# Threshold attention and two FFN layers on one core: value products of later batches moved behind a pair's last tile

## The chip, the cores and the metric

The kernel runs on one core of a Trainium2 chip. The metric is the device time of the whole program in microseconds. Three runs of the kernel before gave a median of 1142.88 us (1142.81 to 1144.38). Besides, one execution was profiled; all rows below come from it.

## The reference, cut to what matters

Four batches of eight heads, 576 positions, 64 channels a head; then two feed-forward layers over 2304 tokens, 512 wide inside and 2048 hidden.

```
scores = scale * q @ k.T                       # per batch and head: 576 x 576
thresh = max(scores, -1) - tau
scores = where(scores >= thresh, scores, -1e9)
attn   = softmax(scores)                       # over the keys
x      = attn @ v                              # 576 x 64 per head, heads side by side: 2304 x 512
h = x @ w_in;  x = (max(h,0) + alpha*min(h,0)) @ w_out
h = x @ w2_in; out = (h * clip(h+3, 0, 6) / 6) @ w2_out
```

## The kernel before

**Attention.** Heads go in pairs, 16 pairs, four to a batch. A pair has nine tiles (`NT = 9`): tile t = 0 to 7 holds 128 queries of one head (head 0 and head 1 in turn), tile 8 the last 64 queries of both. For each tile `do_S` makes the scores (line 377, tile name `s`), `soft` takes the maximum on VectorE, the exponential on ScalarE (`e`) and the threshold with the sum on VectorE, and after each odd tile and after tile 8 `soft_norm` divides on GpSimd and `do_T` transposes the weights on TensorE (`t` at line 439, `r` for the last 64 keys at line 430). ScalarE copies each transpose from PSUM to SBUF (lines 440 and 431, into `p`, or `p1` for tile 8). `do_PV` multiplies with the values (line 470, `pv`), ScalarE copies the product from PSUM to `xo` (line 476), and behind tile 8 DMAs store `xo`.

`do_T` and `do_PV` call 128 queries of both heads a unit; a pair has four units and the 64 queries of tile 8. Before the change one `p` tile holds two units and there are two buffers. In batch 0 each unit is multiplied as soon as it is transposed. In the later batches there are two places per pair: behind tile 3 the first two units (256 columns), behind tile 8 the other two (256 columns) and the 64 of tile 8, side by side in one PSUM tile. Each value product at line 470 is ten matmuls over the keys, which the trace shows as 20 instructions, since the operands are float32. Scores and the FFN run in float32r (shown as f32 too).

**FFN.** Blocks of 512 tokens, one per batch, 16 groups `h` (line 216, 12 matmuls of 512 columns) and 16 groups `o` (lines 245 and 251, also 12 each) per layer. ScalarE, VectorE and GpSimd turn `h` into `m`, `g` and the two halves `gs`, and split the weights into two halves `wi` and `wo`; in the first pass through a layer they also decode them from float64 (lines 148 to 154).

**What sets the order.** The program is written as one loop over the 144 tiles; from three tiles behind batch 0 on, groups of the FFN queue are added at a fixed pace, about 1.8 a tile. A scheduler then puts the instructions of each engine in an order, by priorities: the steps of a tile stand 50 places higher, `do_PV` of batch 0 100 places. Each engine works through its list in order. PSUM is split into `ps_s` (scores, two tiles), `ps_t` (transposes, two banks) and `ps_ho` with two banks, in which `pv`, `h`, `o` and some `pt` (transposes of q and k, line 322) take turns in the order in which the program is written. So a value product keeps its place among the FFN groups, while scores and transposes may run ahead of it as far as `e` (four buffers) and `p` allow.

Behind the last pair the rest of the queue runs, and then a last FFN stage over batch 3 and the left-over queries, with six PSUM banks for `o` and two for `h`.

Of the kernel before, what the change touches and what calls it, by code (L numbers as in the profile page):

```python
# [9 lines left out]
F32 = mybir.dt.float32  # L10
# [9 lines left out]
P = 128  # L20
# [12 lines left out]
def kernel(  # L33
# [13 lines left out]
    nc = tc.nc  # L47
    B, H, S, D = q.shape
# [4 lines left out]
    SM = 512  # L53
    SR = S - SM
# [364 lines left out]
    def do_T(n, t, first):  # L419
        e, _ = st["e"]  # L420
        if n == 1:
            pt = a3.tile([P, 1, NB + 1, P], F32, tag="p1", name="p1", bufs=1)
        elif t % 4 == 1:
            pt = a3.tile([P, 2, 2 * NB + 1, P], F32, tag="p", name="p", bufs=2)
        else:
            pt = st["p"][0]
        dst = pt[:, t % 4 // 2 if n == 2 else 0]
# [15 lines left out]
        st["p"] = st.get("p", []) * (t % 4 != 1) + [pt] * (n == 1 or t % 4 == 1)  # L443


    def do_PV(i):
# [3 lines left out]
        if b == 0:  # L450
            parts = [(1, st["p"][1], 0)] if t == NT - 1 else [(2, st["p"][0], t % 4 // 2)]
        elif t in (3, NT - 1):
            parts = [(2, st["p"][0], None)] + [(1, p1, 0) for p1 in st["p"][1:]]
        else:
            return
        pv = ps_ho.tile([P, SM], F32, tag="ho", name="pv")
        at = 0
        for n, pt, u in parts:
            m = SR if n == 1 else P if u is not None else 2 * P
            for kt in range(NB + 1):  # L460
                for h in (1, 0) if b == 0 else (0, 1):
                    blk = n * NB if kt == NB else kt + NB * h * (n - 1)
                    o = pv[64 * h:64 * h + 64, at:at + m]
                    if n == 1:
                        r = pt[:, 0, blk, SR * h:SR * h + m]
                    elif u is None:
                        o, r = o.rearrange("p (u q) -> p u q", u=2), pt[:, :, blk, :]
                    else:
                        r = pt[:, u, blk, :]
                    nc.tensor.matmul(o, lhsT=vn[:, h, kt, :], rhs=r, start=(kt == 0 and at == 0), stop=(kt == NB), skip_group_check=True)  # L470
            at += m
        if "xo" not in st[pi]:
            st[pi]["xo"] = a2.tile([P, S], F32, tag="xo", name="xo")
        xo = st[pi]["xo"]
        end = S if t == NT - 1 else t // 2 * P + P
        nc.scalar.copy(xo[:, end - at:end], pv[:, 0:at])
# [237 lines left out]
```

## Time and profile before

| | before |
|---|---|
| median of three runs | 1142.88 us |
| the profiled execution: time, span | 1142.49 us, 1140.7 us |
| TensorE (PE) matmul busy | 1099.5 us, 96% of the span |
| VectorE (DVE), ScalarE (ACT), GpSimd (POOL) busy | 609.1, 692.3, 682.5 us |
| granted TensorE clock, mean | 0.998 |
| value products, line 470, 1120 instructions | 90.0 us busy |

The time is read off TensorE: where another engine is late, TensorE stands still, and where it does not stand still the time is the sum of what its matmuls take from start to start. Batch 0 alone takes the first 117 us or so, the mixture of attention and FFN lasts to about 845 us, and the last stage of the FFN takes the rest.

### The profile page before, as it was taken

To read this page: it belongs to the slowest core of one execution; us is meant where nothing else is said; L and a number is where in the kernel's file an instruction comes from. 1 tells how busy PE (TensorE), PEld (TensorE's weight loads), DVE (VectorE), ACT (ScalarE), POOL (GpSimd) and SP (SyncE) were. 2 spreads that over 40 slices of the span, in tenths; PEclk is the share of its full clock that TensorE was granted. 3 is DMA by queue.
4 is the path that set the end of the run, shared out by engine and by line. 5 is a ranking of instruction groups with operands and counts; after the bars stand their busy time and mean duration, and the time that the engine had idled before them with its cause. 6 is when DMAs were issued, how large, how long until landed. Compare 5 with 4: busy or idle time off the path is not lost.

```text
span 1140.7 us, 18515 instructions
## 1 busy us (share of the span) xinstructions
PE 1099.5 (96%) x6464; PEld 909.3 (80%) x6464; DVE 609.1 (53%) x1215; ACT 692.3 (61%) x1316; POOL 682.5 (60%) x726
## 2 busy tenths in 40 slices
PE   6888999999999999999999999999999999999997
PEld 5677788787777788888878888887778888888886
DVE  6889778988897535463555445362334222232121
ACT  6899889888887655466656565564444333344332
POOL 3877779988888755556556656454344434344432
PEclk9999999999999999999999999999999999999999
DMA  5536456666765432333333432322234222212201
GB/s 166 170 114 202 118 166 223 217 213 208 224 217 177 143 103 85 106 106 98 105 107 116 150 95 64 102 65 85 82 101 160 65 65 65 66 56 65 65 28 56
DMA packets 92765, 137.44 MB, mean 120 GB/s; under 512 B 19328, under 2 KB 48512, under 8 KB 92672
## 3 DMA queue, kind: packets, MB, share of 16 engines
q1 hardware_dynamic: 92672, 136.26, 39.6%
q8 instruction: 51, 0.84, 0.3%
q14 instruction: 42, 0.34, 0.1%
HBM read 101.72 MB, written 25.17 MB: 111 GB/s over the span
## 4 chain that ended last, share of the span: by engine, by line
PE 80%; ACT 6%; DVE 5%; DMA 3%; issue 3%; POOL 2%; SPq 0%; POOLq 0%; DVEq 0%; ACTq 0%
PE h L216 32%; PE o L245 14%; PE o L251 14%; PE pv L470 6%; PE s L377 5%; PE t L439 4%; PE r L251 2%; PE r L245 2%; DVE nmx L398 1%; PE pt L322 1%; ACT e L399 1%; DVE e L401 1%; ACT p L440 1%; DMA raw<-in_k_dram 1%; DMA wo<-f 1%
## 5 line engine op out<-in xcount | busy, mean ns | idle before, releaser
L216 PE MATMUL h<-x,wi 128*128 128x512 f32 (+1 forms) x1536 | 357.3, 381 | 1.7 <-DVE thr L400 1.7
L216 PEld LDWEIGHTS h<-x,wi 128*128 128x128 f32 x1536 | 271.7, 188 | 56.1 <-ACT wi L101 1.9
L241 POOL TENSOR_TENSOR gs<-g,gs 128x512 fp32r<-128x512 f32 (+1 forms) x160 | 192.9, 1207 | 161.8 <-ACT gs L237 160.0
L251 PE MATMUL o<-wo,gs 128*128 128x512 f32 x768 | 193.6, 396 | 3.4 <-DVE g L231 1.5
L245 PE MATMUL o<-gs,wo 128*128 128x512 f32 x768 | 194.2, 397 | 0.3
L251 PEld LDWEIGHTS o<-wo,gs 128*128 128x128 f32 x768 | 140.6, 188 | 35.7 <-DVE g L231 2.9
L245 PEld LDWEIGHTS o<-gs,wo 128*128 128x128 f32 x768 | 140.1, 188 | 29.1 <-DVE g L223 0.9
L231 DVE SCALAR_TENSOR_TENSOR g<-m,h 128x512 f32<-128x512 f32 x80 | 50.6, 632 | 163.5 <-ACT m L229 159.7
L399 ACT ACTIVATE e<-s,nmx 128x576 f32<-128x576 f32 x144 | 107.8, 753 | 48.7 <-DVE nmx L398 47.9
L401 DVE SCALAR_TENSOR_TENSOR e<-s,thr,e 128x576 f32<-128x576 f32 x144 | 116.0, 814 | 37.9 <-ACT e L399 36.9
L223 DVE SCALAR_TENSOR_TENSOR g<-m,rest_sb,h 128x512 f32<-128x512 f32 x80 | 55.4, 693 | 145.0 <-ACT m L221 134.1
L102 POOL TENSOR_TENSOR wi<-st,wi 128x512 fp32r<-128x512 f32 x56 | 72.3, 1292 | 100.4 <-ACT wi L101 100.3
L398 DVE TENSOR_REDUCE nmx<-s 128x1 f32<-128x576 f32 x144 | 106.9, 751 | 45.3 <-PE s L377 44.9
L413 POOL TENSOR_SCALAR e<-e,rc 128x576 f32<-128x576 f32 x144 | 113.2, 798 | 28.7 <-DVE rc L410 25.4
L237 ACT CAST gs<-g 128x512 fp32r<-128x512 f32 (+1 forms) x160 | 93.4, 584 | 34.3 <-DVE g L231 13.1
L229 ACT ACTIVATE m<-h,three 128x512 f32<-128x512 f32 x80 | 51.7, 647 | 102.6 <-PE h L216 100.8
L377 PE MATMUL s<-ka,qt 128*128 128x288 f32 x512 | 97.6, 318 | 7.6 <-DVE thr L400 3.1
L101 ACT CAST wo<-st 128x512 fp32r<-128x512 f32 x96 | 57.3, 620 | 75.2 <-DMA st<-wo 62.8
L221 ACT ACTIVATE m<-h 128x512 f32<-128x512 f32 x80 | 44.5, 556 | 92.9 <-PE h L216 92.4
L102 POOL TENSOR_TENSOR wo<-st,wo 128x512 fp32r<-128x512 f32 x56 | 74.4, 1347 | 39.9 <-ACT wo L101 39.7
L440 ACT COPY p<-t 128x512 f32<-128x512 f32 x144 | 83.3, 598 | 23.3 <-PE t L439 12.4
L470 PE MATMUL pv<-p,v 128*64 128x256 f32 (+2 forms) x1120 | 90.0, 310 | 4.4 <-ACT p L440 4.0
(88 smaller groups left out, 1599.1 us busy)
## 6 DMA issues: line engine op xcount, KB each, us to landing
st<-wi SPq DMA_DIRECT2D x96, 256.0 KB, 2.7
st<-wo SPq DMA_DIRECT2D x96, 256.0 KB, 2.7
raw<-in_moe_w_in_dram SPq DMA_DIRECT2D x32, 512.0 KB, 4.3
raw<-in_moe_w_out_dram SPq DMA_DIRECT2D x32, 512.0 KB, 3.8
ka<-ka SPq DMA_DIRECT2D x30, 304.0 KB, 4.2
wi<-f SPq DMA_DIRECT2D x32, 256.0 KB, 3.0
wo<-f SPq DMA_DIRECT2D x32, 256.0 KB, 3.2
raw<-in_k_dram SPq DMA_DIRECT2D x16, 256.0 KB, 4.1
```

What stands on the lines that cost most here:

```text
L102: lo_eng.tensor_tensor(out=lo, in0=src, in1=f32(hi), op=ALU.subtract)
L216: nc.tensor.matmul(h[:, :n], lhsT=w[:, ws, kt * P:(kt + 1) * P], rhs=x[:, xs, kt, :n], start=(i == 0), stop=(i == len(steps) - 1))
L241: nc.gpsimd.tensor_tensor(out=gs[:, 1, :n], in0=g[:, :n], in1=f32(gs[:, 0, :n]), op=ALU.subtract)
L245: nc.tensor.matmul(o[:, :n], lhsT=w[:, ws, dt * P:(dt + 1) * P], rhs=gs[:, gsel, :n], start=fresh and start and i == 0, stop=stop and i == ...
L251: nc.tensor.matmul(o[:m, :], lhsT=gs[:, gsel, tt * P:tt * P + m], rhs=w[:, ws, :], start=start and i == 0, stop=stop and i == 2)
L377: nc.tensor.matmul(ps[:, half, 0:SH], lhsT=w, rhs=s["k"][:, a, c + half * SH:c + half * SH + SH], start=(n == 0), stop=(n == len(mms) - 1))
L398: nc.vector.tensor_reduce(out=nmx, in_=ps, axis=AX.XY, op=ALU.max, negate=True)
L399: nc.scalar.activation(eh, ps, AF.Exp, bias=nmx, scale=1.0)
L401: nc.vector.scalar_tensor_tensor(out=eh, in0=ps, scalar=thr, in1=eh, op0=ALU.is_ge, op1=ALU.mult, accum_out=sm[:, h:h + 1])
L413: nc.gpsimd.tensor_scalar(out=eh, in0=eh, scalar1=rc[:, h:h + 1], scalar2=0.0, op0=ALU.mult, op1=ALU.add)
L440: nc.scalar.copy(dst[:, h * NB:h * NB + NB], ps)
L470: nc.tensor.matmul(o, lhsT=vn[:, h, kt, :], rhs=r, start=(kt == 0 and at == 0), stop=(kt == NB), skip_group_check=True)
```

## The change

`p` becomes one tile with all four units of a pair, in one buffer instead of two of half the size. In batch 0 the products stay where they are. In later batches the first three pairs of each batch have no product behind tile 3 any more; behind tile 8 they multiply all four units at once, 512 queries in one PSUM bank, and the 64 of tile 8 in a second bank. The last pair of each batch keeps its product behind tile 3, and takes a second bank for the 64 of tile 8 too. Both products of tile 8 are issued before their copies to `xo`.

```diff
@@ do_T
-        elif t % 4 == 1:
-            pt = a3.tile([P, 2, 2 * NB + 1, P], F32, tag="p", name="p", bufs=2)
+        elif t == 1:
+            pt = a3.tile([P, 4, 2 * NB + 1, P], F32, tag="p", name="p", bufs=1)
...
-        dst = pt[:, t % 4 // 2 if n == 2 else 0]
+        dst = pt[:, t // 2 if n == 2 else 0]
...
@@ do_PV
-        elif t in (3, NT - 1):
-            parts = [(2, st["p"][0], None)] + [(1, p1, 0) for p1 in st["p"][1:]]
+        elif t == 3 and hp == NP - 1:
+            parts = [(2, st["p"][0], slice(0, 2))]
+        elif t == NT - 1:
+            parts = [(2, st["p"][0], slice(2 * (hp == NP - 1), 4)), (1, st["p"][1], 0)]
...
-        pv = ps_ho.tile([P, SM], F32, tag="ho", name="pv")
-        at = 0
+        pvs = []
         for n, pt, u in parts:
-            m = SR if n == 1 else P if u is not None else 2 * P
+            pv = ps_ho.tile([P, SM], F32, tag="ho", name="pv")
+            units = isinstance(u, slice)
+            m = SR if n == 1 else (u.stop - u.start) * P if units else P
...
-        end = S if t == NT - 1 else t // 2 * P + P
-        nc.scalar.copy(xo[:, end - at:end], pv[:, 0:at])
+            at = SM if n == 1 else (u.start if units else u) * P
+            pvs.append((pv, at, m))
+        for pv, at, m in pvs:
+            nc.scalar.copy(xo[:, at:at + m], pv[:, 0:m])
```

The order of the instructions follows from the scheduler. First TensorE's list around the end of the third pair of batch 2 (the profiled execution reaches it at about 415 us); `v_192` is one of the two value tiles. Before:

```order
L245 MATMUL o<-gs,wo 128x512 x12
L377 MATMUL s<-ka,qt 128x288 x6
L470 MATMUL pv<-p,v_192 64x256 x10
L470 MATMUL pv<-p_5355,v_192 64x64 x10
L245 MATMUL o<-gs,wo 128x512 x12
L430 MATMUL r<-ident,e 128x128
L322 MATMUL pt<-identr,nat 128x128 x3
L216 MATMUL h<-x,wi 128x512 x24
```

And of the change, at the same place among the FFN groups:

```order
L216 MATMUL h<-x,wi 128x512 x12
L245 MATMUL o<-gs,wo 128x512 x12
L476 MATMUL pv<-p,v_192 64x512 x10
L476 MATMUL pv<-p_5305,v_192 64x64 x10
L245 MATMUL o<-gs,wo 128x512 x12
L430 MATMUL r<-ident,e 128x128
L322 MATMUL pt<-identr,nat 128x128 x3
L216 MATMUL h<-x,wi 128x512 x24
```

The product keeps its place, with 512 columns in place of 256, and the `o` group stands directly behind the product of tile 8 in both. Of the nine products with 512 columns eight are followed in this way; in the first one, scores and transposes stand between and behind its parts.

ScalarE's list at the same place, before (the `p<-t` pair is the next pair's third unit):

```order
L529 ACTIVATE acc<-o 128x512
L399 ACTIVATE e<-s,nmx 128x576
L440 COPY p<-t 128x512 x2
L476 COPY xo<-pv 128x320
L237 CAST gs<-g 128x512
L101 CAST wo<-st 128x512 x3
```

And of the change (the `p<-t` pair is the next pair's first unit):

```order
L533 ACTIVATE acc<-o 128x512
L480 COPY xo<-pv 128x512
L440 COPY p<-t 128x512 x2
L480 COPY xo<-pv 128x64
L237 CAST gs<-g 128x512
L101 CAST wo<-st 128x512 x3
```

The copy of the product is now in two parts, the larger ahead of the two copies of transposes.

TensorE's list at the end of batch 0 (about 112 to 124 us), before:

```order
L470 MATMUL pv<-p_1691,v_195 64x64 x10
L377 MATMUL s<-ka,qt 128x288 x4
L439 MATMUL t<-ident,e 128x128 x8
L430 MATMUL r<-ident,e 128x128
L377 MATMUL s<-ka,qt 128x288 x4
L322 MATMUL pt<-identr,nat 128x128 x6
L325 MATMUL pt<-identr,nat 128x64
L377 MATMUL s<-ka,qt 128x288 x4
L439 MATMUL t<-ident,e 128x128 x8
L470 MATMUL pv<-p,v_192 64x256
L430 MATMUL r<-ident,e 128x128
L216 MATMUL h<-x,wi 128x512 x12
```

And of the change:

```order
L476 MATMUL pv<-p_1687,v_195 64x64 x10
L216 MATMUL h<-x,wi 128x512 x3
L377 MATMUL s<-ka,qt 128x288 x4
L439 MATMUL t<-ident,e 128x128 x4
L216 MATMUL h<-x,wi 128x512 x8
L439 MATMUL t<-ident,e 128x128 x4
L216 MATMUL h<-x,wi 128x512 x10
L430 MATMUL r<-ident,e 128x128
```

The first FFN groups now start directly behind the last product of batch 0. Up to that place TensorE's list is the same in both. Counted over the whole list, in pieces of one kind in a row, TensorE has 1022 rows before and 1037 in the change; it goes from float32 work (`t`, `r`, `pv`) to float32r work (all else) 211 times before and 210 times in the change.

## Rows read from the trace of the kernel before

**Rows 1.** Page, busy time, share and instructions of each engine.

```profile
PE 1099.5 (96%) x6464; PEld 909.3 (80%) x6464; DVE 609.1 (53%) x1215; ACT 692.3 (61%) x1316; POOL 682.5 (60%) x726
```

**Rows 2.** Busy time by stretch; last columns clock, DMA share, GB/s.

```profile
core 0: us, PE busy (x) PEld busy (x) DVE busy (x) ACT busy (x) POOL busy (x), PEclk, DMA share, GB/s
...
117.00:400.00 283.00, 275.77 (x1590) 224.72 (x1590) 229.55 (x454) 232.16 (x427) 243.56 (x250) 1.00 0.61 191
400.00:845.00 445.00, 441.33 (x2492) 358.41 (x2491) 207.67 (x402) 246.80 (x469) 247.79 (x250) 1.00 0.34 97
```

**Rows 3.** Waits of PE, 117 to 845 us: total, times, longest.

```profile
PE pt L322 <- ACT p L431: 1.8, 2, 1.6
PE h L216 <- DVE thr L400: 1.7, 1, 1.7
...
PE pt L322 <- ACT p L440: 1.1, 1, 1.1
...
PE t L439 <- ACT p L431: 0.6, 1, 0.6
```

**Rows 4.** Timeline of PE: start, duration, instruction; value products and their successors.

```profile
46.59 1.31 PE L470 MATMUL pv<-p,v 128*64 128x128 f32 x20
47.84 0.45 PE L322 MATMUL pt<-identr,nat 128*128 128x128 f32 x3
...
446.54 2.38 PE L470 MATMUL pv<-p,v 128*64 128x256 f32 x20
448.85 0.80 PE L377 MATMUL s<-ka,qt 128*128 128x288 f32 x4
449.48 2.91 PE L245 MATMUL o<-gs,wo 128*128 128x512 f32 x12
...
419.48 2.96 PE L470 MATMUL pv<-p,v 128*64 128x256 f32 x40
422.37 3.02 PE L245 MATMUL o<-gs,wo 128*128 128x512 f32 x12
```

**Rows 5.** Timeline of PE: FFN matmuls with 512 columns.

```profile
150.42 3.00 PE L216 MATMUL h<-x,wi 128*128 128x512 f32 x12
153.26 0.60 PE L439 MATMUL t<-ident,e 128*128 128x128 f32 x4
```

**Rows 6.** Timeline of PE: scores that follow float32r work.

```profile
224.71 0.69 PE L377 MATMUL s<-ka,qt 128*128 128x288 f32 x4
225.25 2.91 PE L245 MATMUL o<-gs,wo 128*128 128x512 f32 x12
```

**Rows 7.** Timeline of ACT behind the product of 419.48 us.

```profile
421.90 1.07 ACT L440 COPY p<-t 128x512 f32<-128x512 f32 x2 [1.31 <-PE pv L470]
422.86 0.44 ACT L476 COPY xo<-pv 128x320 f32<-128x320 f32 x1
423.36 0.62 ACT L237 CAST gs<-g 128x512 fp32r<-128x512 f32 x1
```

**Rows 8.** Timeline, batch 0: TensorE waits for a copy of a product.

```profile
48.13 0.26 ACT L476 COPY xo<-pv 128x128 f32<-128x128 f32 x1
...
48.44 0.36 PE L322 MATMUL pt<-identr,nat 128*128 128x128 f32 x2 [0.16 <-ACT xo L476]
```

**Rows 9.** Timeline of PE at the end of batch 0.

```profile
115.08 0.33 PE L430 MATMUL r<-ident,e 128*128 128x128 f32 x1 [0.24 <-ACT p L440]
...
119.39 0.65 PE L470 MATMUL pv<-p,v 128*64 128x256 f32 x2 [0.48 <-ACT p L440]
```

**Rows 10.** Waits, whole span: ScalarE's copies of transposes for a product.

```profile
ACT p L440 <- PE pv L470: 10.7, 9, 1.7
```

**Rows 11.** Groups by line and shape: busy, mean ns, idle before, releasers.

```profile
L440 ACT COPY p<-t 128x512 f32<-128x512 f32 x144 | 83.3, 598 | 23.3 <-PE t L439 12.4 <-PE pv L470 10.7
```

More of the change, by code (lines that the diff above doesn't have):

```diff
@@ L442, in do_T @@
             rest()
-        st["p"] = st.get("p", []) * (t % 4 != 1) + [pt] * (n == 1 or t % 4 == 1)
+        st["p"] = st.get("p", []) * (t != 1) + [pt] * (n == 1 or t == 1)
     def do_PV(i):
@@ L450, in do_PV @@
         if b == 0:
[L451 to L453 removed]
+            parts = [(1, st["p"][1], 0)] if t == NT - 1 else [(2, st["p"][0], t // 2)]
+        elif t == 3 and hp == NP - 1:
+            parts = [(2, st["p"][0], slice(0, 2))]
+        elif t == NT - 1:
+            parts = [(2, st["p"][0], slice(2 * (hp == NP - 1), 4)), (1, st["p"][1], 0)]
         else:
             return
[L456 to L457 removed]
+        if "xo" not in st[pi]:
+            st[pi]["xo"] = a2.tile([P, S], F32, tag="xo", name="xo")
+        xo = st[pi]["xo"]
+        pvs = []
         for n, pt, u in parts:
[L459 removed]
+            pv = ps_ho.tile([P, SM], F32, tag="ho", name="pv")
+            units = isinstance(u, slice)
+            m = SR if n == 1 else (u.stop - u.start) * P if units else P
             for kt in range(NB + 1):
@@ L462, in do_PV @@
                     blk = n * NB if kt == NB else kt + NB * h * (n - 1)
-                    o = pv[64 * h:64 * h + 64, at:at + m]
+                    o = pv[64 * h:64 * h + 64, 0:m]
                     if n == 1:
                         r = pt[:, 0, blk, SR * h:SR * h + m]
-                    elif u is None:
-                        o, r = o.rearrange("p (u q) -> p u q", u=2), pt[:, :, blk, :]
+                    elif units:
+                        o, r = o.rearrange("p (u q) -> p u q", q=P), pt[:, u, blk, :]
                     else:
                         r = pt[:, u, blk, :]
[L470 to L474, printed above, removed]
-        end = S if t == NT - 1 else t // 2 * P + P
-        nc.scalar.copy(xo[:, end - at:end], pv[:, 0:at])
+                    nc.tensor.matmul(o, lhsT=vn[:, h, kt, :], rhs=r, start=(kt == 0), stop=(kt == NB), skip_group_check=True)
+            at = SM if n == 1 else (u.start if units else u) * P
+            pvs.append((pv, at, m))
+        for pv, at, m in pvs:
+            nc.scalar.copy(xo[:, at:at + m], pv[:, 0:m])
         if t < NT - 1:
```

## Prediction

> **What bounds the kernel now.** I read the page's busy line first [rows 1]: PE holds 1099.5 of 1140.7 us, no other engine more than 61%. That is an average, so next the windows by stage [rows 2]: between 117 and 400 us PE is busy for 275.77 of 283 us, between 400 and 845 us for 441.33 of 445 us, at a clock column of 1.00 (the 2.4 GHz level). The change works in these two stages, and PE stands still there for 7.23 + 3.67 = 10.9 us. So there are just two ways to gain: matmul work that takes less time from start to start, or a part of those 10.9 us. Then I read who ends PE's waits there [rows 3]: the four entries shown make 5.2 us, in few and single waits, 1.7 us at most; three of them are transposes that wait until ScalarE has emptied `ps_t`. ScalarE in turn waits for value products nine times, 10.7 us in all [rows 10]: copies of the next pair's third unit wait until the `p` buffer is free. These waits mostly cost PE nothing, since it is at work on the product itself.
>
> **The change part by part.**
>
> *The product itself.* Streams get longer, columns stay. A block of 20 instructions takes 47.84 - 46.59 = 1.25 us with 128 columns and 448.85 - 446.54 = 2.31 us with 256 [rows 4], so 1.06 us for each further 128 columns. On that line 512 columns take 2.31 + 2 x 1.06 = 4.43 us, against 2 x 2.31 = 4.62 us in two blocks: 0.19 us less. There is no row with 512 columns in a value product. The bounds: FFN matmuls with 512 columns take (153.26 - 150.42) / 12 = 0.237 us each [rows 5], so 20 of them 4.73 us, 0.11 us more than the two blocks; the other end is the two blocks' stream without any fixed part, 4 x 1.06 = 4.24 us, 0.38 us less. The line is of the same operation and lies nearer. Nine pairs of twelve change: -1.7 us (from -3.4 to +1.0).
>
> A rule of the Trainium skill gives another size here. *TensorE: Matmul & The Clock Gate*, section Back-to-back issue gap, gives an isolated matmul N / 2.4 + 2.5 ns on a warm array; by it a pair of 256-column instructions costs only 2.5 ns more than one of 512, and the saving would be 20 x 2.5 ns = 0.05 us a pair, 0.5 us in all, an estimate from that page. The trace differs from it: 2.31 us / 20 is 115 ns, where the formula has 109 ns [rows 4].
>
> *Entering and leaving the block.* A change between float32 and float32r costs PE time. Four score matmuls take 225.25 - 224.71 = 0.54 us behind float32r work [rows 6] and 449.48 - 448.85 = 0.63 us behind a product [rows 4]: 0.09 us. Nine blocks fewer would save some 0.09 us on either side, 9 x 2 x 0.09 = 1.6 us, if all else stood still. It doesn't: the counted changes between the two types are 211 before and 210 after, and PE's list has 15 pieces more, since the scheduler cuts FFN groups and transposes differently. So I take -0.1 us, and keep -1.6 and, for 15 pieces at 0.09 us, +1.4 us as bounds.
>
> *Two banks in place of one.* This speaks against the change. `ps_ho` has two banks. Before, the product took one and the `o` group behind it had the other: at 422.37 us PE goes on without a wait [rows 4]. Now the 512 columns take one, the 64 the other, and the `o` group behind needs the first back; so it waits for the copy of 512 columns. What I can work out: the block of 256 and 64 columns takes 422.37 - 419.48 = 2.89 us, of which 2.31 is the 256 part, so the 64 part starts at 421.79 us. ScalarE, which stood waiting, starts the first copy at 421.90 us [rows 7], 0.11 us later. A copy of 512 columns takes 0.60 us [rows 11], and PE resumes 0.05 us behind a copy: 48.13 + 0.26 = 48.39 against 48.44 us [rows 8]. So the bank is back 0.11 + 0.60 + 0.05 = 0.76 us after the 64 part starts, and that part takes 2.89 - 2.31 = 0.58 us: PE waits 0.18 us. This meets eight of the nine pairs (in the first one, scores stand between the two products); the last pair of a batch copies only 256 columns. +1.4 us. Bounds: 0, if the part of 64 columns takes longer than I read; and +0.76 us x 8 = +6.1 us if ScalarE is late each time by as much as one more copy of 0.60 us.
>
> The Trainium skill has this as a rule: *Perfetto Trace Analysis*, section Matmuls under Optimizing Tensor Performance, asks that independent groups of matmuls rotate through PSUM banks so that emptying one overlaps the next group, and adds that larger matmuls are the more efficient. The first half speaks against the change and the second for it. By the second alone the sum would hold the -1.7 us without the +1.4 us.
>
> *The copies themselves.* ScalarE now copies 512 and 64 columns in place of 256 and 320. It waits for longer (the block ahead is two times as long), and `gs` and `wo` stand behind it. Before, the `gs` cast started at 423.36 us, 1.0 us behind the block's end [rows 7]; now 0.60 us of `xo` lies ahead of the two transposes' 1.07 us and some 0.2 us behind, so `gs` starts about 0.3 us later against the block's end. What hides that is the `o` group and the first FFN group behind it, 2.8 us each by [rows 5], for which inputs are there: 0. If that cover were gone it would be 0.3 us for each of nine pairs, 2.7 us.
>
> *One `p` buffer.* The next pair's transposes can fill both `ps_t` banks and no more until the product is done, where before two further units could be copied. The front of the attention then stands still behind each product and catches up in the FFN's company. Before, PE's waits for `ps_t` cost 1.8 + 1.1 + 0.6 = 3.5 us [rows 3]. I can't read from any row whether the new order has more or fewer of them: 0, with bounds of -3.5 us (all gone) and +7.9 us (one more of the mean, 3.5 us / 4 = 0.88 us, for each of nine pairs). In batch 0 a unit's product stands in PE's list ahead of the next pair's transposes, so the single buffer costs nothing there.
>
> *The end of batch 0.* FFN matmuls now fill two waits of 0.24 and 0.48 us [rows 9]: -0.7 us. Bounds: -0.7 and 0, if the FFN's first inputs come too late.
>
> **Sum.** -1.7 - 0.1 + 1.4 + 0 + 0 - 0.7 = -1.1 us. The profiled execution took 1142.49 us (its span 1140.7 and 1.8 us around it), so 1141.4 us. The median of the runs, 1142.88 us, lies 0.4 us higher; on its scale the forecast is 1141.8 us. That is no change that a measurement of this kernel can tell: 0.2% are 2.3 us, so "same" is 1140.6 to 1145.2 us.
>
> **The rivals.**
>
> *The hand-over of the bank costs nothing and the blocks' edges count.* Then -1.7 - 1.6 - 0.7 = -4.0 us: 1138.9 us. For it: in 0.18 us of calculated wait there is little room, and PE stands still for 10.9 us in the two stages, which any new order deals out anew. Against it: 211 and 210 changes of type.
>
> *The single buffer makes waits (the other sign).* Behind each product the next pair's copies, scores and transposes come in a crowd; a transpose that stands in PE's list ahead of FFN work holds PE until ScalarE has emptied a `ps_t` bank. At 0.88 us for each of nine pairs the sum is -1.1 + 7.9 = +6.8 us: 1149.7 us; it decides the sign from four such waits, 3.5 us, which lead from 1141.8 to 1145.3 us. For it: three of the four longest entries of [rows 3] are of this kind, and GpSimd and ScalarE are at 86% and 82% between 117 and 400 us [rows 2]. Against it: from 400 us on ScalarE is at 55%, and the copies waited for products before too without PE standing still [rows 10].
>
> *The bank comes back late.* As above, but with ScalarE behind by one more instruction in the first passes, where decoding stands in its list: 0.6 us for four pairs, +2.4 us: 1144.2 us, still "same".
>
> **How the numbers follow.** Forecast with the late bank included, 1140.6 to 1145.2 us: 0.45. The first rival and whatever else shortens the waits: 0.31. The single buffer with four such waits or more, 1145.3 to 1149.7 us: 0.24. So faster 0.31, same 0.45, slower 0.24. The likeliest time is 1141.8 us, the forecast's own range 1140.6 to 1144.2. For 8 in 10 the range reaches down to 1138.0 us, a little under the first rival (1138.9), and up to 1147.5, between six and seven of the nine waits (1141.8 + 6.5 x 0.88).
>
> **What would show it.** Right: nine blocks of 20 instructions with 512 columns at about 4.4 us; behind the 64 columns an `o` group with about 0.2 us of idle time, ended by line 480; 10 to 12 us without PE work between 117 and 845 us. Wrong: 512-column blocks near 4.7 us; no such idle time; transposes and `pt` with more than 3.5 us of waits for lines 431 and 440; or PE idle in the first passes for GpSimd or ScalarE.

## The result and the profile after

| | before | after |
|---|---|---|
| median of the runs | 1143.62 us (6 runs, 1141.81 to 1145.47) | 1152.37 us (6 runs, 1151.7 to 1153.47) |
| profiled execution: time, span | 1142.49, 1140.7 us | 1151.7, 1149.9 us |

The ratio is 1.0081, with a 95% interval of 1.0070 to 1.0091: 8.8 us slower, outside the range of the forecast. The cause has to be read from small differences, since no single wait is 8.8 us long. First the page's busy line, which answers to [rows 1]:

```profile
PE 1104.4 (96%) x6284; PEld 899.0 (78%) x6284; DVE 609.6 (53%) x1215; ACT 694.0 (60%) x1319; POOL 683.4 (59%) x726
```

There are 180 matmul instructions fewer (nine pairs times 20), and yet PE is busy for 4.9 us more; it stands still for 45.5 us in place of 41.2. So about half of the loss is no idle time at all. The windows by stage, as in [rows 2], and two short ones of which more below:

```profile
117.00:400.00 283.00, 271.91 (x1454) 213.83 (x1453) 222.22 (x432) 225.92 (x414) 234.25 (x238) 0.99 0.61 190
400.00:845.00 445.00, 439.74 (x2377) 350.60 (x2376) 213.67 (x422) 253.66 (x483) 254.84 (x260) 1.00 0.34 97
270.30:273.70 3.40, 3.40 (x8) 2.72 (x9) 3.40 (x8) 3.19 (x7) 3.40 (x4) 0.50 0.14 43
181.50:185.00 3.50, 3.46 (x13) 3.10 (x13) 2.50 (x5) 3.23 (x7) 3.33 (x5) 0.51 1.08 383
```

PE's idle time is 11.09 + 5.26 = 16.35 us here, against 10.9 us before. The forecast had named 10 to 12 us as the sign of being right. Who ends the waits, 117 to 845 us, against [rows 3] (total, times, longest):

```profile
PE h L216 <- DVE g L231: 4.4, 4, 2.9
PE t L439 <- ACT qt L342: 3.3, 6, 0.9
PE pt L322 <- ACT p L431: 2.1, 2, 1.6
PE o L245 <- DVE g L223: 1.9, 3, 1.2
PE o L251 <- DVE acc L537: 1.7, 3, 0.8
...
PE o L251 <- DVE g L231: 0.4, 1, 0.4
```

Four entries of the same view of before, which [rows 3] leaves out, are needed beside it:

```profile
PE o L251 <- DVE g L231: 1.5, 3, 1.0
PE o L251 <- DVE acc L533: 1.3, 2, 0.8
...
PE t L439 <- ACT ka L331: 0.7, 1, 0.7
...
PE t L439 <- ACT qt L342: 0.2, 1, 0.2
```

FFN groups that wait for VectorE make 4.4 + 1.9 + 1.7 + 0.4 = 8.4 us, against 1.7 + 1.5 + 1.3 = 4.5 us before: this kind grew most. The second entry needs care. A transpose `t` of the weights doesn't use `qt`; it waits for a bank of `ps_t`, which from the second pair of batch 1 on also holds the transposed q (`pt`), until ScalarE has copied that to `qt` (line 342; to `ka` for k, line 331). Waits for `ps_t` by way of lines 431 and 440, which the prediction counted, fell from 3.5 to 2.1 us; with lines 331 and 342 they rose from 4.4 to 5.4 us. So the second rival's kind of wait is there, but it grew by 0.9 us (the entries before rounding) and not by 7.9.

**Where the time is lost.** A matmul's time from its start to the next start can be set against the usual time of the same kind followed by the same kind (the lower quartile over both traces; for products and transposes the mean without the top tenth). Worked out so from all matmul rows, the usual times add up to 1056.0 us before and 1056.5 us after: by this measure the amount of work is the same. What is above usual is 72.4 us before and 81.7 us after, and this difference of 9.3 us is the difference of the spans, 9.2 us. Followed along equal amounts of usual work, the changed kernel is 2.9 us ahead at 128 us, 7.4 us behind at 394 us, and 9.3 us behind at the end. So 10.3 us are lost between 128 and 394 us, in the FFN's first passes where the weights are decoded, and some 2 us behind them. The last stage adds nothing. The measure has a blind spot: work that is cut into pieces in one of the traces alone is in part its own usual (see the cut product below).

**A wait from near.** PE's timeline from 266 us (start, duration, instruction, idle time before it and its releaser):

```profile
266.17 1.22 PE L377 MATMUL s<-ka,qt 128*128 128x288 f32 x8
270.30 7.28 PE L216 MATMUL h<-x,wi 128*128 128x512 f32 x24 [2.92 <-DVE g L231]
277.43 1.23 PE L377 MATMUL s<-ka,qt 128*128 128x288 f32 x8
```

And the same 24 matmuls undisturbed, in the same trace:

```profile
430.21 5.72 PE L216 MATMUL h<-x,wi 128*128 128x512 f32 x24
435.77 0.36 PE L322 MATMUL pt<-identr,nat 128*128 128x128 f32 x3
```

The longest wait after the change costs twice. PE stands still for 2.92 us. Then the 24 matmuls take 277.43 - 270.30 = 7.13 us, where 435.77 - 430.21 = 5.56 us is usual, since the granted clock is 0.50 (the 1.2 GHz level) from 270.3 to 273.7 us: 1.6 us more. The chain behind the wait, ScalarE and VectorE at the same time:

```profile
266.17 0.82 ACT L148 ACTIVATE low<-raw 128x513 uint16<-128x513 uint32 x1 [1.08 <-POOL f L154]
266.85 0.65 ACT L229 ACTIVATE m<-h,three 128x512 f32<-128x512 f32 x1
267.41 0.60 ACT L101 CAST wi<-f 128x512 fp32r<-128x512 f32 x1
267.92 0.68 ACT L229 ACTIVATE m<-h,three 128x512 f32<-128x512 f32 x1
```

```profile
268.16 1.41 DVE L398 TENSOR_REDUCE nmx<-s 128x1 f32<-128x576 f32 x2
269.49 1.27 DVE L231 SCALAR_TENSOR_TENSOR g<-m,h 128x512 f32<-128x512 f32 x2
```

ScalarE's `m` stands behind a decoding step (`low`) that waits 1.08 us for GpSimd; the `g` that needs `m` stands on VectorE behind two maxima of scores; and PE's next `h` waits for the bank that `g` reads last. Every engine is in its listed order, and none is the bound; the order has put decoding, attention and FFN one behind the other. No step of this chain is a value product, a `p` buffer or a copy of `xo`.

**A loss that is no wait.** In the first pair of batch 1 the product of 512 columns comes in seven pieces of 2, 6, 2, 2, 2, 4 and 2 instructions, with transposes between them. PE's timeline, the first two pieces and the sixth:

```profile
148.67 1.07 PE L476 MATMUL pv<-p,v 128*64 128x512 f32 x2
149.67 0.33 PE L430 MATMUL r<-ident,e 128*128 128x128 f32 x1
149.93 1.93 PE L476 MATMUL pv<-p,v 128*64 128x512 f32 x6
151.79 0.33 PE L439 MATMUL t<-ident,e 128*128 128x128 f32 x1
...
155.84 1.08 PE L476 MATMUL pv<-p,v 128*64 128x512 f32 x4
156.85 0.33 PE L430 MATMUL r<-ident,e 128*128 128x128 f32 x1
```

From its start to the next instruction's, a piece of two takes 149.67 - 148.67 = 1.00 us, one of four 1.01 us, one of six 1.86 us. Each matmul is two instructions, and the program issues the two heads in turn. In a whole block, by the single instructions, they start in pairs 0.007 us apart, and a pair takes 0.43 us; in a piece of two one head stands alone, and its two instructions take 0.48 and 0.52 us. So one head alone took as long as both. The seven pieces take 5 x 1.00 + 1.86 + 1.01 = 7.9 us, where a whole block takes 4.34 us: 3.5 us more. Before, the same pair had one cut too, a piece of 2 ([rows 9], to the next start at 119.96 us) and one of 18:

```profile
119.96 0.33 PE L430 MATMUL r<-ident,e 128*128 128x128 f32 x1
...
123.50 2.37 PE L470 MATMUL pv<-p,v 128*64 128x256 f32 x18
125.80 0.70 PE L322 MATMUL pt<-identr,nat 128*128 128x128 f32 x6
```

There 0.57 + 2.30 = 2.87 us stand against 2.31 us for a whole block, only 0.6 us more. Net of that the pieces cost 3 us, a third of the loss, and all of it is counted as busy time.

### The profile page after: what moved, and what is told of

It is laid out like the page before. It is cut to its first block, busy times and chain, and to the rows that moved or that the text cites. A ratio compares the mean times of both kernels' runs of the same rounds, so it can differ in the third digit from the quotient of the medians.

```text
span 1149.9 us, 18144 instructions
## 1 busy us (share of the span) xinstructions
PE 1104.4 (96%) x6284; PEld 899.0 (78%) x6284; DVE 609.6 (53%) x1215; ACT 694.0 (60%) x1319; POOL 683.4 (59%) x726
## 4 chain that ended last, share of the span: by engine, by line
PE 76%; ACT 7%; DVE 7%; issue 4%; DMA 3%; POOL 2%; SPq 1%; DVEq 0%; ACTq 0%; POOLq 0%
PE h L216 30%; PE o L245 14%; PE o L251 12%; PE s L377 5%; PE pv L476 5%; PE t L439 3%; PE r L251 2%; DVE nmx L398 2%; PE r L245 2%; PE pt L322 1%; ACT low L148 1%; DVE low L150 1%; ACT p L440 1%; DVE e L401 1%; ACT e L399 1%
## 5 line engine op out<-in xcount | busy, mean ns | idle before, releaser
L102 POOL TENSOR_TENSOR wi<-st,wi 128x512 fp32r<-128x512 f32 x56 | 72.4, 1295 | 84.4 <-ACT wi L101 83.3
L439 PE MATMUL t<-ident,e 128*128 128x128 f32 x576 | 90.0, 279 | 6.7 <-ACT p L431 3.4
L476 PE MATMUL pv<-p,v 128*64 128x128 f32 (+3 forms) x940 | 90.7, 335 | 3.5 <-ACT p L440 3.3
```

What stands on the lines that cost most here:

```text
L102: lo_eng.tensor_tensor(out=lo, in0=src, in1=f32(hi), op=ALU.subtract)
L439: nc.tensor.transpose(ps[:, kt], e[:, c:c + P], ident)
```

## The experiments

In the tables "lines" is the number of rows by which TensorE's list of instructions differs from that of before (line and buffer numbers left out; 1022 rows there), and "PE busy" is that between 117 and 400 us, 275.77 us before. Each ratio is against before on the same chip, with its 95% interval.

### Parts of the change

**One `p` buffer alone.** The products stay as before; `p` is one tile of four units, one buffer.

```diff
-        elif t % 4 == 1:
-            pt = a3.tile([P, 2, 2 * NB + 1, P], F32, tag="p", name="p", bufs=2)
+        elif t == 1:
+            pt = a3.tile([P, 4, 2 * NB + 1, P], F32, tag="p", name="p", bufs=1)
...
-                        o, r = o.rearrange("p (u q) -> p u q", u=2), pt[:, :, blk, :]
+                        o, r = o.rearrange("p (u q) -> p u q", u=2), pt[:, 2 * (t > 3):2 * (t > 3) + 2, blk, :]
```

> The kernel before with one p tile of four units in one buffer; the products stay where they were (256 columns behind tile 3, 256 and 64 behind tile 8 in one bank). If the single buffer makes the loss (theory A: the front of the attention stands still behind each product, its work then comes in a crowd, and FFN inputs come late in the first passes), this kernel loses most of it: +6 to +9 us against before, with the waits of h, o and t between 180 and 290 us as in the change. If the later product and its second bank make it (theory B), this kernel is within 2 us of before. If a wait in one place, which any new order may or may not have, makes it (theory C), it is anywhere between, and a wait of 2 us or more with a lower granted clock behind it is in the trace exactly when the time is high.

**Two banks alone.** The kernel before, with a bank of its own for the 64 queries.

```diff
-        pv = ps_ho.tile([P, SM], F32, tag="ho", name="pv")
...
         for n, pt, u in parts:
+            pv = ps_ho.tile([P, SM], F32, tag="ho", name="pv")
...
+            pvs.append((pv, at, m))
...
+        for pv, u, m in pvs:
+            nc.scalar.copy(xo[:, end - at + u:end - at + u + m], pv[:, 0:m])
```

> The kernel before with the 64 columns of tile 8 in a PSUM bank of their own, copied apart; all else as before. The copy of 256 columns takes 0.37 us, so the bank is back 0.11 + 0.37 + 0.05 = 0.53 us after the 64 part starts, which itself takes 0.58 us: hardly a wait. Theories A and C: within 1.5 us of before. Theory B (the second bank makes the loss): +3 us or more.

**The change with two blocks of 256 columns** in the one bank in place of one of 512.

```diff
+            halves = [slice(c, c + 2) for c in range(u.start, u.stop, 2)] if units else [u]
+            for i2, w in enumerate(halves):
+              for kt in range(NB + 1):
...
+                        o = pv[64 * h:64 * h + 64, 2 * P * i2:2 * P * i2 + 2 * P].rearrange("p (u q) -> p u q", q=P)
+                        r = pt[:, w, blk, :]
```

> The change, but the 512 columns are issued as two blocks of 256 into the same bank. Streams: 2 x 2.21 against 4.34 us for nine pairs, +0.7 us against the change. All theories: like the change within 1.5 us, unless the order of the scheduler moves a wait (theory C), which then shows in the trace. It tells what the width itself is worth.

**The change in batches 2 and 3 only;** batch 1 multiplies behind tile 3 as before.

```diff
-        elif t == 3 and hp == NP - 1:
+        elif t == 3 and (b == 1 or hp == NP - 1):
...
-            parts = [(2, st["p"][0], slice(2 * (hp == NP - 1), 4)), (1, st["p"][1], 0)]
+            parts = [(2, st["p"][0], slice(2 * (b == 1 or hp == NP - 1), 4)), (1, st["p"][1], 0)]
```

> The change, but in batch 1 every pair keeps its product behind tile 3 as the last pair of a batch does; p has one buffer throughout. Batch 1 lies beside the first FFN passes (about 117 to 360 us). Theory A: the single buffer still holds the front, so little comes back, 1149 to 1153 us. Theory B (the late wide product is what hurts): the loss in the first passes goes, 1145 to 1148 us. Theory C: the loss goes exactly if the wait of 2.9 us near 270 us is gone.

| kernel | median, its before | ratio | lines | PE busy |
|---|---|---|---|---|
| one `p` buffer alone | 1148.94, 1143.8 | 1.0045 (1.0031 to 1.0059) | 572 | 273.52 |
| two banks alone | 1142.81, 1143.8 | 0.9993 (0.9984 to 1.0002) | 93 | 276.73 |
| two blocks of 256 | 1148.01, 1143.8 | 1.0045 (1.0031 to 1.0059) | 626 | 271.64 |
| batch 1 as before | 1150.67, 1143.8 | 1.0062 (1.0049 to 1.0075) | 535 | 272.10 |

The single buffer alone brings 5.1 us, with every product as before. Along equal usual work, as above, it is 0.2 us behind at 161 us and 5.1 us at 391 us, and stays there: lost in the same stretch as in the change. The waits of its profile, 117 to 845 us:

```profile
PE t L439 <- ACT qt L342: 4.4, 6, 2.2
PE h L216 <- DVE g L231: 1.5, 3, 1.0
PE o L245 <- DVE g L223: 1.4, 3, 0.7
PE o L251 <- DVE acc L533: 1.2, 2, 0.8
PE t L439 <- ACT p L431: 0.9, 1, 0.9
```

The first and the last are waits for `ps_t`, the first by way of the transposed q; the others are FFN groups that wait for VectorE. Theory A had 6 to 9 us for this kernel and theory B at most 2, and both missed. The sign that theory C gave, a wait of 2 us or more with a lower granted clock behind it exactly when the time is high, missed as well: the one wait of 2.2 us has none behind it.

A second bank costs nothing while the block ahead of the 64 has 256 columns. Its copy is short enough to be done under the 64 block, as PE's timeline shows by 421.92 - 419.03 = 2.89 us, the same as in [rows 4]:

```profile
419.03 2.96 PE L470 MATMUL pv<-p,v 128*64 128x256 f32 x40
421.92 3.02 PE L245 MATMUL o<-gs,wo 128*128 128x512 f32 x12
```

The block's width is worth next to nothing: from the single instructions, two blocks of 256 in one bank take 4.367 us and one of 512 takes 4.343 us. Yet this kernel as a whole, expected within 1.5 us of the change, is 4.5 us nearer to before. And leaving batch 1 as before, where the loss begins, brings back only 1.9 us, as theory A had it and theory B not; the wait of 2.9 us is gone there and most of the loss is not, so theory C's sign missed again. Part of that is the cut product: with two blocks the first pair's product has a whole block of 256 columns and pieces of 2, 14 and 4 instructions, together 5.2 us, 2.7 us less than the 7.9 us of the change. Where batch 1 is as before, the seven pieces are gone too. The other differences don't follow from the edits; three of the four have a TensorE list that differs in over 500 lines. So the next question was whether the rest is the room in `p`, or the new order.

### Room in `p` or a new order

**The buffer freed by units.** As the single buffer alone and as the whole change, but `p` is one tile for the whole program, so that a unit can be written as soon as its own product is done, not when the whole tile is.

```diff
+    p_all = a1.tile([P, 4, 2 * NB + 1, P], F32, tag="p", name="p")
...
-            pt = a3.tile([P, 4, 2 * NB + 1, P], F32, tag="p", name="p", bufs=1)
+            pt = p_all
```

> As e1 (one p tile of four units, products as before), but the tile is allocated once for the whole kernel, so that a unit's copy waits only for the last product that read this unit, not for the whole pair. Layout, sizes and products are those of e1; only the time at which a unit is free differs. Theory A (the front waits because nothing of p is free before the pair's last product): the loss of e1 goes, within 1.5 us of before, and the transposes' waits for qt and p go back to those of before. If it were the layout or anything else in the single tile: like e1, +5 us.

> The change with the p tile allocated once, as in e9. The product of 512 columns reads all four units behind tile 8, so the next pair's first unit still waits for it; only the pairs behind a batch's last one get two units early. Theory A: still most of the loss, +5 to +9 us, and about 0.2 us at each of eight hand-overs of the bank. If the loss were due to the release of the whole tile alone: within 2 us of before.

**Half of `p`:** the kernel before with `bufs=1` for `p`, two units in all.

```diff
-            pt = a3.tile([P, 2, 2 * NB + 1, P], F32, tag="p", name="p", bufs=2)
+            pt = a3.tile([P, 2, 2 * NB + 1, P], F32, tag="p", name="p", bufs=1)
```

> The kernel before with one p buffer of two units instead of two: the units behind tile 3 wait for the product of the first two. Still less room for the front than in e1. Theory A: the loss of e1 or more, +5 to +10 us against before, with more waits of transposes for qt and p. If the room in p did not matter: within 2 us of before.

**More of `p`:** three buffers of two units, with room made by one `nat` tile in place of two and one `xo` buffer; and as its control that room made, with two `p` buffers.

```diff
-            t = a1.tile([P, n, 2, D], F32R, tag="natq", name="natq")
...
+        t = a1.tile([P, n, 2, D], F32R, tag="nat", name="nat")
...
-            pt = a3.tile([P, 2, 2 * NB + 1, P], F32, tag="p", name="p", bufs=2)
+            pt = a3.tile([P, 2, 2 * NB + 1, P], F32, tag="p", name="p", bufs=3)
...
+            st[pi]["xo"] = a2.tile([P, S], F32, tag="xo", name="xo", bufs=1)
```

> The kernel before with three p buffers of two units in place of two. The room comes from a tile that only the first pair uses (its q is split into the same tile as k now) and from the second xo buffer, which costs something at the start and perhaps at the stores (see the control e13). Theory A carried further: with more room the front runs farther ahead, and the waits between 117 and 845 us fall: 0 to -4 us against the control. If two buffers are already enough, no change within 1 us against the control.

> Control for e12: the kernel before without the extra tile and with one xo buffer, two p buffers as before. All theories: +0.5 to +3 us against before, all of it at the start, since the first pair's q is split only when the transposes of k are through with the tile.

| kernel | median, its before | ratio | lines | PE busy |
|---|---|---|---|---|
| one `p`, freed by units | 1143.83, 1143.45 | 0.9999 (0.9990 to 1.0008) | 155 | 272.81 |
| the change, freed by units | 1152.85, 1143.45 | 1.0076 (1.0061 to 1.0091) | 581 | 270.70 |
| half of `p` | 1158.23, 1143.45 | 1.0120 (1.0104 to 1.0136) | 634 | 268.48 |
| three `p` buffers | 1146.48, 1143.66 | 1.0028 (1.0017 to 1.0040) | 521 | 272.22 |
| its control | 1142.74, 1143.66 | 0.9996 (0.9987 to 1.0004) | 26 | 275.76 |

Halving the room is dear, 14.8 us, more than theory A expected. One tile that is freed by units costs nothing where the single buffer cost 5.1 us, as theory A had it. The change with a `p` freed in the same way is as slow as the change, so the release of the whole tile isn't what makes it slow; but its product of 512 columns reads all four units, so the next pair's first unit waits for it all the same, and the run doesn't speak against the room. It has the seven pieces of the change, too. More room than before is slower, by 2.8 us, where theory A expected a gain, while its control, expected to lose a little, loses nothing. So the room alone doesn't decide. What goes with the time is the column of lines: the kernels whose list stays near that of before are as fast as before, the others are not. The busy time goes with it less well; the first row is at 272.81 us there and yet as fast. These runs can't part room and order, since the scheduler makes the order from the buffers: where one of these edits changed the room, the order changed with it.

### New orders with `p` left alone

**Attention earlier or the FFN faster against it.** `LAG`, by which the FFN queue starts behind batch 0, from 3 tiles to 2; or the pace of the queue times 1.02. Each also with the single `p` buffer of the first experiment.

```diff
-    LAG = 3
+    LAG = 2
```

```diff
-    per = len(queue) / max(1, NS - PB)
+    per = 1.02 * len(queue) / max(1, NS - PB)
```

> The kernel before with the FFN queue started one tile earlier (2 tiles behind batch 0 in place of 3). p, its buffers, the products and all sizes are those of before; the order on TensorE differs in 610 lines, as much as in the slow kernels. Theory A (room in p): within 2 us of before. Theory C (any new order loses, since that of before is a fortunate one): +3 us or more.

> The kernel before with FFN groups added at a pace 2% faster. p, its buffers, the products and all sizes are those of before; the order on TensorE differs in 586 lines. Theory A: within 2 us of before. Theory C: +3 us or more.

> As n3_earlier, with the one p tile of e1 in one buffer. Theory A: +3 to +8 us against n3_earlier. Theory C: as n3_earlier within 3 us, on either side.

> As n5_faster, with the one p tile of e1 in one buffer. Theory A: +3 to +8 us against n5_faster. Theory C: as n5_faster within 3 us, on either side.

**The tiles' priority** from 50 to 80 places; and a slot of the FFN queue: of four `o` groups in a row, three have an `h` group behind them, and the one without, the third (`d` = 2), becomes the second (`d` = 1) or the fourth (`d` = 3).

```diff
-        with tc.high_priority(offset=50):
+        with tc.high_priority(offset=80):
```

```diff
-                if d != 2:
+                if d != 1:
```

> The kernel before with the steps of a tile 80 places higher in priority in place of 50; the program is else the same, the order on TensorE differs in 202 lines. Theory C in its strict form (any new order loses): +2 us or more. If only the pace and place of FFN against attention matter (theory D, which n3 and n5 changed): within 2 us of before.

> The kernel before with the h group that is left out among four o groups left out behind the second in place of the third; the order on TensorE differs in 249 lines, the work and the pace are the same. Theory C: +2 us or more. Theory D: within 2 us of before.

> As m9, but left out behind the fourth o group; the order differs in 429 lines. Theory C: +3 us or more. Theory D: within 2 us of before.

| kernel | median, its before | ratio | lines | PE busy |
|---|---|---|---|---|
| `LAG` 2 | 1150.21, 1144.31 | 1.0050 (1.0037 to 1.0064) | 610 | 271.42 |
| the same, one `p` buffer | 1148.87, 1144.31 | 1.0039 (1.0025 to 1.0054) | 656 | 272.46 |
| pace 1.02 | 1152.49, 1144.31 | 1.0076 (1.0061 to 1.0091) | 586 | 271.29 |
| the same, one `p` buffer | 1156.78, 1144.31 | 1.0112 (1.0095 to 1.0129) | 643 | 269.41 |
| priority 80 | 1145.59, 1144.14 | 1.0012 (1.0002 to 1.0022) | 202 | 274.86 |
| slot 1 | 1145.68, 1144.14 | 1.0014 (1.0004 to 1.0023) | 249 | 275.44 |
| slot 3 | 1155.14, 1144.14 | 1.0099 (1.0084 to 1.0114) | 429 | 272.23 |

None of these touches the products, and only the second and fourth touch `p`. An FFN that is dealt in one tile earlier costs 5.9 us, a pace 2% faster 8.2 us, a slot moved by one 11.0 us: sizes like that of the change. The priority and slot 1 cost about 1.5 us each, just clear of the noise: under the 2 us that theory C asked for, and within the 2 us of theory D, which slot 3 then missed by far. So a new order can cost nearly nothing, or as much as the change. Lag and pace also change how much of the FFN stands beside the attention; the slots change the order alone.

On the first of these orders the single buffer makes the time 1.3 us shorter, which the intervals don't tell from nothing, on the second 4.3 us longer, and on that of before 5.1 us longer. Theory C had within 3 us for both and theory A 3 to 8 us, so each is right once. The buffer's price doesn't hold from one order to another, but on two of the three it is 4 to 5 us.

The waits of slot 3, 117 to 845 us, show once more a mixture, and another one:

```profile
PE o L251 <- DVE g L231: 3.5, 4, 1.9
PE o L251 <- DVE acc L533: 1.8, 3, 0.8
PE pt L322 <- ACT p L440: 1.4, 1, 1.4
PE h L216 <- DVE g L231: 1.3, 1, 1.3
```

### The hand-over of the bank

**The 64 ahead of the 512,** so that the small bank is copied under the large block; and **the copy of 512 columns split** between ScalarE and VectorE.

```diff
-            parts = [(2, st["p"][0], slice(2 * (hp == NP - 1), 4)), (1, st["p"][1], 0)]
+            parts = [(1, st["p"][1], 0), (2, st["p"][0], slice(2 * (hp == NP - 1), 4))]
```

```diff
         for pv, at, m in pvs:
+            if m == SM:
+                nc.vector.tensor_copy(xo[:, at + m // 2:at + m], pv[:, m // 2:m])
+                m = m // 2
             nc.scalar.copy(xo[:, at:at + m], pv[:, 0:m])
```

> The change with the product of 64 columns ahead of that of 512. The o group behind then gets the bank of the 64, which is free long before: no wait at line 245 or 251 for line 480. But the 512 columns now take the bank of the o group ahead of them, which is free only after an addition on VectorE or a copy on ScalarE, 0.11 + 0.69 + 0.05 us, while the 64 columns take 0.68 us: 0.2 us again, now ahead of the 512 columns. Theory A: within 2 us of the change. If the hand-over were the main loss: -3 us or more against the change.

> The change, but the copy of the 512 columns is shared: ScalarE copies the left half, VectorE the right half, so that the bank is back after about 0.11 + 0.37 + 0.05 us, within the 0.68 us of the 64 columns, if VectorE is free. The part of 64 columns then takes 0.68 us to its successor in place of 0.88 in most of eight places: up to -1.5 us against the change, give or take what a new order does. If the hand-over of the bank were the main loss: 5 us less than the change or better.

| kernel | median, its before | ratio | lines | PE busy |
|---|---|---|---|---|
| the 64 first | 1161.48, 1143.45 | 1.0155 (1.0138 to 1.0172) | 672 | 265.88 |
| the copy split | 1156.34, 1143.66 | 1.0109 (1.0093 to 1.0124) | 619 | 270.25 |

The first was expected within 2 us of the change and the second up to 1.5 us below it, and both are slower than it, by 9 and 4 us. Neither tells what the hand-over costs, since its order is new again.

The change freed by units answers it better, on PE at 427 us:

```profile
427.10 5.09 PE L477 MATMUL pv<-p,v 128*64 128x512 f32 x40
432.13 0.33 PE L431 MATMUL r<-ident,e 128*128 128x128 f32 x1
```

There `r`, which needs no bank of `ps_ho`, stands behind the 64, and the products take 432.13 - 427.10 = 5.03 us to their successor, 0.19 us less than in the change. It is so at all eight of its whole blocks, where 0.2 us of waiting had been expected at each. This kernel has no hand-over there and is as slow as the change, so the hand-over isn't what most of the loss is made of.

No version beat the kernel before: the two fastest, two banks alone and the control, can't be told from it.

## Why the prediction was wrong

**The product itself: right for eight pairs, wrong for one.** The pair's end in the changed kernel, PE and then ScalarE:

```profile
421.82 5.09 PE L476 MATMUL pv<-p,v 128*64 128x512 f32 x40
427.04 3.02 PE L245 MATMUL o<-gs,wo 128*128 128x512 f32 x12
```

```profile
426.40 0.59 ACT L480 COPY xo<-pv 128x512 f32<-128x512 f32 x1 [3.88 <-PE pv L476]
426.88 1.08 ACT L440 COPY p<-t 128x512 f32<-128x512 f32 x2
427.84 0.24 ACT L480 COPY xo<-pv 128x64 f32<-128x64 f32 x1
428.04 0.62 ACT L237 CAST gs<-g 128x512 fp32r<-128x512 f32 x1
```

Both blocks take 427.04 - 421.82 = 5.22 us, of which, by the single instructions, 4.34 are the 512 columns (forecast 4.43) and 0.88 the 64. Without the hand-over a pair's products take 4.34 + 0.68 = 5.02 us, against 2.31 + 2.89 = 5.20 us by [rows 4]: 0.18 us less for each of the eight pairs with a whole block, 1.4 us. That is the forecast's size and its reason: 0.15 us come from not leaving and entering a block between the halves, 0.02 us from the width. But the forecast counted nine pairs. In the first one the product takes 7.9 us in seven pieces, where its two blocks of 256 columns took 2.87 + 2.21 = 5.1 us before: 2.8 us more. So the term was +1.4 us and not -1.7. The list on record ahead of the prediction shows other work between the parts of this product, and the prediction says that the scheduler cuts differently; it priced a piece at 0.09 us, where these cost about 0.5 us each.

**Entering and leaving: a wrong reading.** The 0.09 us belong to the value product and not to the change of type. Transposes (`t`) are float32 as well. In the trace of before, four of them between FFN matmuls take, with one FFN matmul ahead and one behind, 0.90 us from start to start (16 places, by median), and the steps inside rows of one kind add up to 2 x 0.23 + 4 x 0.11 = 0.90 us: no cost for two changes of type. So the count of 211 and 210 changes of type says nothing about this cost, and the saving for nine blocks is one with the fixed part of the term above.

**Two banks in place of one: right.** ScalarE's copy of 512 columns ends at 426.99 us, and `o` starts at 427.04 us, 0.05 us behind, as worked out. The 64 block takes 0.88 us to its successor, where it takes 0.68 us when its bank is not waited for: 0.20 us at seven pairs and 0.18 us at one (forecast 0.18), together 1.6 us (forecast 1.4). The timeline prints no idle time there, since the modelled end of the block comes close to the start of `o`; it is read from the starts. At the eight whole blocks gain and hand-over cancel, as in the sum.

**The end of batch 0: right in sign.** By the account along equal work the changed kernel is 2.9 us ahead at 128 us, more than the 0.7 us; but some 0.9 us of it is a stretch of slower clock that the profiled execution of before has and the other hasn't (last section).

**The copies: 0, not shown wrong.** `gs` starts 1.0 us behind the block's last start-to-start (428.04 against 427.04), where before it was 1.0 us too [rows 7]; the late `gs` of 0.3 us did not appear here, because the block itself ends later by the hand-over.

**The failing steps** are two terms of the sum. The first is "One `p` buffer", put as "I can't read from any row whether the new order has more or fewer of them: 0", and with it the sentence in the first rival that any new order deals out PE's waits anew. I took a new deal to be as likely to gain as to lose, and priced it by waits for `ps_t` alone. Between 117 and 845 us PE stood still for 5.45 us more, which is inside the term's bounds and far from its 0; 3.9 us of that is FFN groups that wait for VectorE, a kind which the term didn't have. [rows 3] had led there: it shows four waits, three of them for `ps_t`, but the third and fourth longest of that view, 1.5 and 1.3 us, are FFN groups that wait for VectorE. The second failing step is "Nine pairs of twelve change: -1.7 us" in "The product itself", where the cut product of the first pair makes it +1.4 us.

**Orders.** Of the eighteen kernels that were run beside the change, the fifteen whose TensorE list differs from before in over 200 lines are all slower, by 1.4 to 18 us, thirteen of them, those with over 400 lines, by 2.8 us or more; the three with 26 to 155 lines can't be told from before. Five of those fifteen leave the products and `p` alone and lose 1.4, 1.5, 5.9, 8.2 and 11.0 us. So in this neighbourhood a new order has a price of its own, no mean of zero. The price doesn't grow smoothly with the lines (429 lines cost 11.0 us, 521 cost 2.8 us), so the share of it in the change, with 631 lines, can't be read off them.

The second rival had the sign and, with 1149.7 us, nearly the size, and that was luck in the main: its waits for `ps_t` grew by 0.9 us of its 7.9. What it says of the single buffer is not refuted, since the buffer alone brings 5.1 us on the order of before.

**What the loss is made of** in the profiled execution, against the sum: PE's idle time between 117 and 845 us, +5.45 us; the clock (two half-clock stretches of 1.6 us each between 117 and 400 us, where before has none in this stage), +3.2 us; the products, +1.4 us, with 0.2 us more for the 64 columns of the first pair, which are cut too; the hand-over, +1.6 us; the start, -2.9 us. These make 9.0 of the 9.2 us of span, with small overlaps that I did not part (the wait of 0.48 us in [rows 9] is in two of them). The waits ahead of 181 and 270 us with the slow clock behind them make 7.7 us; the two longest waits of before in this stage, 1.63 and 1.74 us, have no slow clock behind them. Over all timed runs the clock tells less: its mean was 0.9966 in 81 runs of before and 0.9950 in six of the change, and (1 - 0.9966) x 1142 = 3.9 us against (1 - 0.9950) x 1150 = 5.8 us, so about 1.9 of the 8.8 us. The kernel with batch 1 as before has no such stretch behind batch 0, and slot 3 neither, and they are 6.9 and 11.0 us slower: waits alone can do it.

**What stays open.** Why the order of before is better than its neighbours isn't shown; the chain at 270 us shows how one wait comes about, not why the mean goes one way. How the change's 5.45 us of waiting divide between less room in `p` and the new order that comes with it isn't shown: the order controls show that an order alone can cost as much, the single buffer cost 5.1, 4.3 and about 0 us on three orders. All eighteen kernels stand beside one order, and if that one was itself picked as the fastest of many, losing is what its neighbours would do; the record has nothing on where it came from. A change with the first pair left as before and no other edit, which would price the cut product by time, was not run, and two buffers of four units neither.

## What to carry to other kernels

Where one engine is busy for 96% and a scheduler sets the order of all, an edit has two prices: the local one, which rows give to a tenth of a microsecond (here -1.4 and +1.6 us at the whole blocks), and that of the new order, which was 1.4 to 11.0 us where nothing else changed, and never a gain that could be measured. Look in the list for blocks that the new order cuts, and price each piece by a row: here seven pieces of one block cost 3.5 us. Count how far the bounding engine's list differs, and before crediting or blaming the edit run controls that change the order and nothing else: a pace, a priority, a slot. A resource's price is only shown when it holds on a second order. A list of waits that leaves entries out can hide the kind that will grow. And the stage where the loss lies (here 128 to 394 us, with GpSimd and ScalarE busy for some 86% and 82% before, against 56% and 55% behind it) says where to look first.

## What the runs showed of the hardware

The granted clock can fall to its lower level after a wait of PE, or not, after the same wait. At the end of batch 0 TensorE's list is the same in both kernels. Before, and then after the change, PE at 107 us:

```profile
106.90 0.66 PE L439 MATMUL t<-ident,e 128*128 128x128 f32 x4 [1.95 <-ACT p L431]
...
108.50 2.40 PE L470 MATMUL pv<-p,v 128*64 128x128 f32 x20
```

```profile
107.18 0.66 PE L439 MATMUL t<-ident,e 128*128 128x128 f32 x4 [2.00 <-ACT p L431]
...
108.52 1.31 PE L476 MATMUL pv<-p,v 128*64 128x128 f32 x20
```

The same wait, 1.95 and 2.00 us, and the product behind it takes 2.40 us in one and 1.31 us in the other. The window of before around it:

```profile
107.90:111.30 3.40, 3.40 (x26) 2.79 (x25) 3.21 (x8) 2.88 (x6) 2.00 (x4) 0.50 0.69 246
```

The stretch is 3.4 us long, at 0.50, and begins a microsecond behind the wait's end. After the change the product that follows this place starts at 111.52 us in place of 112.43 us. The two stretches after the change, at 181.5 and 270.3 us, stand behind waits of 1.61 and 2.92 us; the waits of 1.6 and 1.7 us in [rows 3] have none behind them. So such a wait cost its own length, and sometimes 1 to 1.6 us on top, and the trace of one execution doesn't tell how often.

A float32 value product of 512 columns took 4.343 us / 20 = 0.217 us an instruction, and two of 256 columns 4.367 us / 40 = 0.109 us, so that a stream twice as long was worth 0.02 us a block in one bank. The other 0.15 of the 0.18 us a pair came from blocks that no longer have to be entered and left apart. What a product costs most is other work between the two heads: one head's matmul of 512 columns alone took 1.00 us, both heads' side by side 1.01 us.
